# Loading q, k and f of the first three units by token and turning them with full-width transpositions

## The chip, the cores and the metric

The kernel runs on one core of a Trainium2 chip. Its time is the device time of one execution in microseconds; the median of three runs is compared. A profile is one such execution, and its span goes from the first to the last instruction. TensorE (PE) multiplies matrices and writes to PSUM; VectorE (DVE), ScalarE (ACT) and GpSimd (POOL) work on SBUF and PSUM; SyncE (SP) and ACT issue transfers (DMA).

## What is computed

A recurrent attention block is followed by a gated feed-forward block, all in float32:

```
B, H, S, D = 4, 8, 768, 48
f = 1 / (1 + exp(-f_logit))
for t in range(S):
    state = f[:, :, t, :, None] * state + einsum('bhd,bhe->bhde', k[:, :, t], v[:, :, t])
    y[:, :, t] = einsum('bhd,bhde->bhe', q[:, :, t], state)
x = y.transpose(0, 2, 1, 3).reshape(3072, 384)
h = x @ w_in                                  # 384 x 2048
out = (h / (1 + exp(-1.702 * h))) @ w_out     # 2048 x 384
```

## The kernel before

The 4 x 768 tokens are cut into 12 units of 256 tokens (`U`); a unit has two halves of 128 tokens (`HALF`, called f = 1 and f = 0). `attention(n)` builds the work of unit n as a list of parts. `f`, `q` and `k` of a unit come in with token and head dimension in the wrong place: they have to be turned, so that the head dimension (48, in slots of 64) lies on the partitions and tokens lie along the free dimension. The result goes to `F` (the gates) and to slots of `X` (q and k).

In attention, six levels l = 0..5 combine blocks of 1, 2, 4, ... 32 tokens. A level copies keys aside (`set_aside`, tile `Kc`, line 494, ACT), forms scores on PE (`score`, line 425), multiplies q and k by running products of the gates (`promote`, line 519, DVE; the products `tot` are formed on POOL, line 416) and writes masked scores to `A` (lines 466 to 485). `turn_k` (line 595) transposes k back on PE. Then state and output `y` follow (lines 534, 643, 689), `y` is copied to `yT` and sent by DMA to `xT`, which the feed-forward products read (lines 1100 and 1114).

`load_raw(n, j)` loads one of f_logit, q, k (j = 0, 1, 2) into the tile `raw`, which has one place for each j and so is loaded anew only after the turn of the unit before. `turn(j, ...)` turns it. Both have two ways: from unit 3 on (`n >= N_FILL`) DVE transposes blocks of 32 x 32; for units 0, 1 and 2 PE does it. Only the second way is changed.

For those three units a partition of `raw` holds 8 following tokens of one head pair, 384 floats for each of two heads (1536 bytes in a row in memory), one DMA for each of the four head pairs, 32 partitions each. `turn` takes one token of the 8 at a time: for each head a product of 64 columns of `raw` with the identity puts 64 partitions of a PSUM bank, two heads beside each other. A bank holds 4 of the 8 tokens, and ACT evacuates it in two pieces, one for each half, with the tokens written in groups of 4. q is loaded one token early (`first = s0 - 1`), so at the start of a sequence its row 0 has no source and is zeroed.

`opening()` is a hand-written order for unit 0, with pieces of unit 1 between its levels. On SP it issues f, k, the first weights; then f and k for unit 1, v, q for unit 1, more weights. ACT issues q of unit 0. On PE: two products with zeros (`keep_up`, line 125), f, k, q of unit 0, then the levels; f of unit 1 is turned in two pieces at levels 2 and 3 (`next_f`), q and k of unit 1 after `turn_k`. Between levels `keep_up(1)` issues a product whose result nobody reads. ACT runs f's sigmoid, then k's evacuation, `Kc`, q's evacuation. Units 1 and 2 are merged with feed-forward products by `merge`, which interleaves a queue of products with the attention parts by share; the weights are decoded in these units by ACT (line 228) and DVE (lines 230 to 233). SP issues each weight load (line 210) when a buffer comes free.

PE and POOL run in the order in which the code is written; up to unit 2 all engines do (`fill_order`). Later a scheduler orders DVE, ACT and SP.

Of the kernel before, what the change touches and what calls it, by code (L numbers as in the profile page):

```python
# [9 lines left out]
F32 = mybir.dt.float32  # L10
I32 = mybir.dt.int32
U32 = mybir.dt.uint32
AF = mybir.ActivationFunctionType
# [10 lines left out]
def kernel(  # L24
# [33 lines left out]
    nc = tc.nc  # L58
    B, H, S, D = q.shape
    DM = H * D  # L60
    DFF = moe_w_in.shape[1]
    P = 128
# [61 lines left out]
    flat_A = A.rearrange("p c f t -> p (c f t)")  # L124
    keep_up(2, 192, (flat_A[:, :P], flat_A[:, :192]))

    R = U // 32
    RW = R * D + HS - D
    raw = const.tile([P, 3, NP, R * D], F32, name="raw")
    by_pair = [raw.rearrange("p j a x -> p j (a x)")[:, j, :2 * RW].rearrange("p (h x) -> p h x", h=2) for j in range(3)]  # L130
    for j in range(3):
        nc.gpsimd.memset(by_pair[j][:, :, R * D:], 0.0)
    nc.gpsimd.memset(by_pair[1][:1, :, :D], 0.0)
    R4 = HALF // 32
    by_half = raw.rearrange("p j a x -> p j (a x)").rearrange("p j (f a x) -> p j f a x", f=2, a=NP)

    ident = const.tile([P, P], F32, name="ident")
    make_identity(nc, ident)
# [1 line left out]

    masks = const.tile([P, NL - 1, 2, 32], F32, name="masks")
    at = [wp.tile([P, n], I32, tag="bits", name=f"at{j}", bufs=PAIRS_AHEAD) for j, n in enumerate((1, (NL - 1) * 64))]
    nc.gpsimd.memset(by_half[:, :, 1, :, R4 * D - 32:], 0.0)
    nc.gpsimd.iota(at[0], pattern=[[0, 1]], base=0, channel_multiplier=1)
    for l, m in enumerate(LEV[:-1]):
        nc.gpsimd.iota(
# [103 lines left out]
    def load_raw(n, j, engines=(nc.sync,)):  # L250
        if n >= NALL:
            return
        b, s0 = n // NU, n % NU * U
        src = (f_logit, q, k)[j]
        first = s0 - (j == 1)

        def span(head, token, dims, d=0):
            return bass.AP(src.tensor, src.offset + ((b * H + head) * S + token) * D + d, dims)
        if n < N_FILL:
            for a in range(NP):  # L260
                engine = engines[a * len(engines) // NP]
                to = by_pair[j][32 * a:32 * (a + 1), :, :R * D]
                if first < 0 and a == 0:

                    for r, rows in ((1, 16), (17, 15)):
                        engine.dma_start(
                            out=to[r:r + rows], in_=span(0, r * R - 1, [[R * D, rows], [S * D, 2], [1, R * D]])
                        )
                    engine.dma_start(out=to[:1, :, D:], in_=span(0, 0, [[R * D, 1], [S * D, 2], [1, (R - 1) * D]]))
                else:  # L270
                    engine.dma_start(out=to, in_=span(2 * a, first, [[R * D, 32], [S * D, 2], [1, R * D]]))
            return
        for f in (1, 0):
            for r in range(4):
                lo = 32 * (r % 2)
                width = R4 * D - lo
                part = span(r // 2, first + (0 if f else HALF), [[R4 * D, 32], [2 * S * D, NP], [1, width]], lo)
                nc.sync.dma_start(out=by_half[32 * r:32 * (r + 1), j, f, :, :width], in_=part)
            if f and first < 0:
                for r in range(4):  # L280
                    lo = 32 * (r % 2)
                    nc.sync.dma_start(
                        out=by_half[32 * r:32 * r + 1, j, f, :, :D - lo],
                        in_=q[b - 1, r // 2::2, S - 1:S, lo:].rearrange("a t d -> t a d"),
                    )
# [33 lines left out]
    def attention(n):  # L319
# [19 lines left out]
        def turn(j, outs, fn=None, pieces=None):  # L339

            if n >= N_FILL:
# [7 lines left out]
                if fn:  # L349
                    fn()  # L350
                return
            for j0 in pieces or range(0, R, 4):
                pt = bank([P, 4, P], f"t_{n}_{j}_{j0}")
                for jj in range(4):
                    for h in range(2):
                        x = (j0 + jj) * D
                        nc.tensor.matmul(  # L357
                            pt[h * HS:(h + 1) * HS, jj, :], lhsT=by_pair[j][:, h, x:x + HS], rhs=ident, start=True, stop=True
                        )
                for f in (1, 0):  # L360
                    at, step = (j0, 1) if f else (HALF - 1 - j0, -1)
                    nc.scalar.activation(
                        view(outs(f), at, [[HALF, NP], [R * step, 16], [step, 4]]),
                        pt.rearrange("p j (a f i) -> p f a i j", a=NP, f=2)[:, 1 - f],
                        (AF.Tanh if n > 1 else AF.Sigmoid) if fn else AF.Copy, scale=0.5 if fn and n > 1 else 1.0,
                    )
            if fn and n > 1:
                half_up()
# [9 lines left out]
        def begin_f(pieces=None):  # L378
            def decay():
                turn(0, lambda f: F[:, ORDER.index(f) * SLOT:(ORDER.index(f) + 1) * SLOT], sigmoid, pieces)  # L380
            if n > N_FILL + 1 and "moved" in copied:
                with tc.issue_after(copied["moved"].ins):
                    decay()
            else:
                decay()
            if n >= N_FILL or (n == 1 and R - 4 in pieces):
                load_raw(n + 1, 0)

        def begin():
# [880 lines left out]
    def opening():  # L1270
# [18 lines left out]
        for l in range(NL):  # L1289
            chosen[:] = [2, 3][l % 2:][:1]  # L1290
            level(l)
            if l in (2, 3):
                next_f((0, 4)[l - 2:][:1])
            elif l < NL - 1:
                keep_up(1)
            if l == 1:
# [75 lines left out]
```

## Time and profile before

| | |
|---|---|
| runs | 599.06, 598.99, 601.0 us; median 599.06 |
| span of the profiled execution | 594.5 us |
| PE busy | 574.9 us, 97% |
| DVE busy | 429.5 us, 72% |
| ACT busy | 291.9 us, 49% |
| POOL busy | 138.4 us, 23% |
| turns by products, line 357 | 288 records, 5.0 to 68.5 us |
| evacuations of them, line 362 | 36 pieces of 128x256, 383 ns each |
| transpositions, line 595 | 4 records in 0.60 to 0.63 us at 60 us |

Every product in float32 shows as two records of weight load and two of matmul, so 144 products at line 357 give 288 matmul records. The duration of a record includes its way through the array; how far apart records start is the rate. Two products of 64 columns each work on the two halves of the array at a time, so their records start at half the distance of full-width ones.

The profiled execution's time is not listed by itself; its span is 4.56 us below the median of the runs, which also count what lies around the span. An idle engine matters only where the chain of waits passes through it.

### The profile page before, as it was taken

To read this page: it belongs to the slowest core of one execution; us is meant where nothing else is said; L and a number is where in the kernel's file an instruction comes from. 1 tells how busy PE (TensorE), PEld (TensorE's weight loads), DVE (VectorE), ACT (ScalarE), POOL (GpSimd) and SP (SyncE) were. 2 spreads that over 40 slices of the span, in tenths; PEclk is the share of its full clock that TensorE was granted. 3 is DMA by queue.
4 is the path that set the end of the run, shared out by engine and by line. 5 is a ranking of instruction groups with operands and counts; after the bars stand their busy time and mean duration, and the time that the engine had idled before them with its cause. 6 is when DMAs were issued, how large, how long until landed. Compare 5 with 4: busy or idle time off the path is not lost.

```text
span 594.5 us, 18457 instructions
## 1 busy us (share of the span) xinstructions
PE 574.9 (97%) x7814; PEld 513.6 (86%) x7814; DVE 429.5 (72%) x696; ACT 291.9 (49%) x613; POOL 138.4 (23%) x214
## 2 busy tenths in 40 slices
PE   6879899999999999999999999999999999999997
PEld 6756776867768789999999999999999999999897
DVE  2898987964866858789778778786887786462284
ACT  4746643453334353474474474573663564452440
POOL 4031200230027216610610700800700602203000
PEclk9979999999999999999999999999999999999999
DMA  7947859840243552353552343553361211001000
GB/s 181 215 124 179 193 145 225 217 100 1 52 106 66 145 130 65 80 139 77 127 146 51 84 113 91 130 134 60 88 168 44 63 38 29 28 3 27 28 1 27
DMA packets 82834, 58.29 MB, mean 98 GB/s; under 512 B 33153, under 2 KB 74785, under 8 KB 82753
## 3 DMA queue, kind: packets, MB, share of 16 engines
q1 hardware_dynamic: 82416, 56.73, 38.9%
q8 instruction: 61, 1.00, 0.7%
q10 hardware_dynamic: 337, 0.39, 0.3%
q14 instruction: 20, 0.16, 0.1%
HBM read 43.98 MB, written 8.39 MB: 88 GB/s over the span
## 4 chain that ended last, share of the span: by engine, by line
PE 87%; DVE 7%; ACT 3%; issue 1%; DMA 1%; POOL 1%; SPq 0%; DVEq 0%; ACTq 0%
PE h L1006 17%; PE h L1100 13%; PE o_Y L869 11%; PE o L1114 10%; PE o_Z L869 8%; PE h_y L1006 6%; PE sc L425 6%; PE o_X L869 4%; PE o_W L869 4%; PE y L689 2%; PE t L357 2%; PE y L534 2%; PE sc L643 1%; DVE X L519 1%; ACT yT L703 1%
## 5 line engine op out<-in xcount | busy, mean ns | idle before, releaser
L1100 PE MATMUL h<-xT,w_in 128*128 128x256 f32 x384 | 89.6, 388 | 1.4 <-DMA xT<-yT 1.4
L523 DVE TENSOR_TENSOR X<-X,tot 128x1024 f32<-128x1024 f32 x45 | 57.0, 1266 | 39.8 <-PE sc L425 33.2
L1100 PEld LDWEIGHTS h<-xT,w_in 128*128 128x128 f32 x384 | 72.8, 193 | 13.8 <-DMA xT<-yT 2.4
L494 ACT COPY Kc<-X 128x512 f32<-128x512 f32 x72 | 48.4, 672 | 65.7 <-DVE X L523 51.5
L1114 PE MATMUL o<-w_out,g 128*128 128x384 f32 x192 | 65.5, 491 | 0.4 <-DVE w_out L233 0.4
L968 POOL TENSOR_TENSOR E<-xT 128x128 f32<-128x128 f32 (+1 forms) x32 | 17.9, 571 | 204.0 <-DMA xT<-yT 112.0
L1114 PEld LDWEIGHTS o<-w_out,g 128*128 128x128 f32 x192 | 35.4, 190 | 22.8 <-DVE w_out L233 1.0
L1006 PE MATMUL h<-E,w_in 128*128 128x128 f32 (+1 forms) x420 | 53.4, 275 | 0.0
L869 PE MATMUL o_Y<-T,S 128*128 128x192 f32 x288 | 50.6, 329 | 0.0
L1006 PEld LDWEIGHTS h<-E,w_in 128*128 128x128 f32 x420 | 50.1, 192 | 0.0
L1036 ACT ACTIVATE g<-g 128x512 f32<-128x512 f32 (+1 forms) x63 | 35.6, 584 | 26.0 <-DVE g L1034 25.3
L1104 ACT ACTIVATE g<-h 128x256 f32<-128x256 f32 x64 | 23.8, 382 | 49.0 <-PE h L1100 48.6
L869 PEld LDWEIGHTS o_Y<-T,S 128*128 128x128 f32 x288 | 46.8, 190 | 0.5
L1034 DVE TENSOR_TENSOR g<-g,h 128x512 f32<-128x512 f32 (+1 forms) x52 | 31.8, 632 | 14.3 <-PE h L1006 13.3
L485 DVE COPY_PREDICATED A<-masks,sc 128x256 f32<-128x256 uint32 (+1 forms) x98 | 42.0, 506 | 0.1
L703 ACT COPY yT<-y 48x256 f32<-48x256 f32 x88 | 32.2, 366 | 18.3 <-PE y L689 17.2
L372 POOL TENSOR_SCALAR F<-F 128x1024 f32<-128x1024 f32 x10 | 17.2, 1716 | 95.9 <-ACT F L375 84.3
L345 DVE STREAM_TRANSPOSE X<-raw 128x512 f32<-128x512 f32 x36 | 38.1, 1105 | 0.1
L425 PEld LDWEIGHTS sc<-X,Kc 48*64 48x64 f32 x1440 | 26.2, 136 | 11.1 <-ACT Kc L494 4.8
L425 PE MATMUL sc<-X,Kc 48*64 48x64 f32 x1440 | 31.0, 222 | 4.8 <-ACT Kc L494 1.9
L1034 DVE TENSOR_TENSOR g<-g,h_y 128x512 f32<-128x512 f32 (+1 forms) x26 | 16.5, 634 | 22.3 <-PE h_y L1006 21.4
L1025 ACT ACTIVATE g<-h 128x512 f32<-128x512 f32 (+1 forms) x46 | 26.1, 576 | 10.8 <-PE h L1006 10.6
(162 smaller groups left out, 1156.2 us busy)
## 6 DMA issues: line engine op xcount, KB each, us to landing
bits<-in_moe_w_out_dram SPq DMA_DIRECT2D x8, 768.0 KB, 7.2
raw<-in_f_logit_dram SPq DMA_DIRECT2D x48, 96.0 KB, 3.5
raw<-in_k_dram SPq DMA_DIRECT2D x48, 96.0 KB, 3.0
bits<-in_moe_w_in_dram SPq DMA_DIRECT2D x8, 576.0 KB
raw<-in_q_dram SPq DMA_DIRECT2D x44, 96.0 KB, 2.3
k_tok<-z SPq DMA_DIRECT2D x56, 64.0 KB, 1.8
kt<-k_tok SPq DMA_DIRECT2D x14, 256.0 KB, 2.8
out_dram<-osb SPq DMA_DIRECT2D x18, 192.0 KB, 2.7
```

What stands on the lines that cost most here:

```text
L345: nc.vector.transpose(view(out, at, [[HALF, NP], [step, R4], [R4 * step, 32]]), by_half[:, j, f].rearrange("p a (j d) -> p (a j) d", j=R4) ...
L425: nc.tensor.matmul(t["sc"][h][g * HS:(g + 1) * HS, a, s, :], lhsT=t["Kc", l][rows(h), x:x + HS], rhs=rhs(h, a, g), start=True, stop=True,)
L485: moved = nc.vector.copy_predicated(out=view(A, c * HALF + at, dims), mask=mask.bitcast(U32), data=got)
L494: nc.scalar.copy(c.rearrange("p (n two m) -> p n two m", two=2, m=m), view(X, KF * SLOT, [[2 * m, SLOT // (2 * m)], [(KR - KF) * SLOT + m, ...
L523: nc.vector.tensor_tensor(x, x, y, ALU.mult)
L703: nc.scalar.copy(view(yT[rows(h)], at, [[U, NP], [step, HS]]), py[columns(h, g), g, :, f, :])
L869: nc.tensor.matmul(t[name], lhsT=lhs(f), rhs=rhs(f), start=(new and i == 0), stop=(i == HF - 1), skip_group_check=True,)
L1006: nc.tensor.matmul(ph[:, t], lhsT=WA[a][:, f * P:(f + 1) * P], rhs=E[n][b], start=(root and t == 0), stop=not goes_on, skip_group_check=True,)
L1034: nc.vector.tensor_tensor(to, to, part, ALU.add if sign > 0 else ALU.subtract)
L1036: nc.scalar.activation(to, to, AF.Gelu_apprx_sigmoid)
L1100: nc.tensor.matmul(ph, lhsT=w_in[:, c, ff * P:(ff + 1) * P], rhs=xTs[n][:, c, :], start=(c == 0), stop=(c == NK - 1))
L1114: nc.tensor.matmul(t["po"], lhsT=g[ff // FG][:, ff % FG, tt * P:(tt + 1) * P], rhs=w_out[:, ff, :], start=(ff == ffs[0]), stop=(ff == ffs[ ...
```

## The change

For units 0 to 2, a partition of `raw` is now a token. It holds two halves (f) of 8 heads, each head in a slot of 64 floats of which 48 come from memory (192 bytes in a row) and 16 are zeroed once by POOL. A load is two DMAs of 128 partitions x 8 heads x 48, first for half f = 1, then for f = 0; at the start of a sequence q's first one leaves out row 0 and is cut into 112 and 15 rows. With a half, four transpositions of 128 x 128 on PE, two heads each, fill one bank, and the bank is the whole half. It is evacuated in one piece of 128x512, the tokens in order (f = 1) or reversed (f = 0). Evacuations are on ACT as before, but in unit 0 both halves of k and half f = 0 of q are on DVE.

```diff
+    R4 = HALF // 32
+    raw = const.tile([P, 3, 2 * NP * R4 * D], F32, name="raw")
+    by_token = raw[:, :, :2 * H * HS].rearrange("p j (f x) -> p j f x", f=2)
+    by_head = by_token.rearrange("p j f (h d) -> p j f h d", h=H)
     for j in range(3):
-        nc.gpsimd.memset(by_pair[j][:, :, R * D:], 0.0)
-    nc.gpsimd.memset(by_pair[1][:1, :, :D], 0.0)
+        nc.gpsimd.memset(by_head[:, j, :, :, D:], 0.0)
+    nc.gpsimd.memset(by_head[:1, 1, 1, :, :D], 0.0)
...
-    nc.gpsimd.memset(by_half[:, :, 1, :, R4 * D - 32:], 0.0)
+    nc.gpsimd.memset(by_half[:, :, 1, 1:, R4 * D - 32:], 0.0)
...
         if n < N_FILL:
-            for a in range(NP):
-                engine = engines[a * len(engines) // NP]
-                to = by_pair[j][32 * a:32 * (a + 1), :, :R * D]
...
-                    engine.dma_start(out=to, in_=span(2 * a, first, [[R * D, 32], [S * D, 2], [1, R * D]]))
+            for i, f in enumerate((1, 0)):
+                engine, t0 = engines[i % len(engines)], first + (0 if f else HALF)
+                for p0, p1 in ((1, 113), (113, P)) if t0 < 0 else ((0, P),):
+                    engine.dma_start(
+                        out=by_head[p0:p1, j, f, :, :D], in_=span(0, t0 + p0, [[D, p1 - p0], [S * D, H], [1, D]])
+                    )
...
-            for j0 in pieces or range(0, R, 4):
-                pt = bank([P, 4, P], f"t_{n}_{j}_{j0}")
-                for jj in range(4):
-                    for h in range(2):
-                        x = (j0 + jj) * D
-                        nc.tensor.matmul(
-                            pt[h * HS:(h + 1) * HS, jj, :], lhsT=by_pair[j][:, h, x:x + HS], rhs=ident, start=True, stop=True
-                        )
-                for f in (1, 0):
-                    at, step = (j0, 1) if f else (HALF - 1 - j0, -1)
+            for f in pieces or (1, 0):
+                pt = bank([P, NP, HALF], f"t_{n}_{j}_{f}")
+                for a in range(NP):
+                    nc.tensor.transpose(pt[:, a, :], by_token[:, j, f, a * P:(a + 1) * P], ident)
+                to = view(outs(f), *((0, [[HALF, NP], [1, HALF]]) if f else (HALF - 1, [[HALF, NP], [-1, HALF]])))
+                if n == 0 and not fn and (j, f) != (1, 1):
+                    nc.vector.tensor_copy(to, pt)
+                else:
                     nc.scalar.activation(
-                        view(outs(f), at, [[HALF, NP], [R * step, 16], [step, 4]]),
-                        pt.rearrange("p j (a f i) -> p f a i j", a=NP, f=2)[:, 1 - f],
-                        (AF.Tanh if n > 1 else AF.Sigmoid) if fn else AF.Copy, scale=0.5 if fn and n > 1 else 1.0,
+                        to, pt, (AF.Tanh if n > 1 else AF.Sigmoid) if fn else AF.Copy, scale=0.5 if fn and n > 1 else 1.0,
                     )
...
-                next_f((0, 4)[l - 2:][:1])
+                next_f((1, 0)[l - 2:][:1])
```

The order of instructions on PE, and on DVE and ACT but for the replaced ones, stays. On SP two small loads of the last token of q come some 20 issues earlier.

More of the change, by code (lines that the diff above doesn't have):

```diff
@@ L125 @@
     keep_up(2, 192, (flat_A[:, :P], flat_A[:, :192]))
[L127 to L130, printed above, removed]
+    R4 = HALF // 32
+    raw = const.tile([P, 3, 2 * NP * R4 * D], F32, name="raw")
+    by_token = raw[:, :, :2 * H * HS].rearrange("p j (f x) -> p j f x", f=2)
+    by_head = by_token.rearrange("p j f (h d) -> p j f h d", h=H)
     for j in range(3):
-        nc.gpsimd.memset(by_pair[j][:, :, R * D:], 0.0)
-    nc.gpsimd.memset(by_pair[1][:1, :, :D], 0.0)
-    R4 = HALF // 32
-    by_half = raw.rearrange("p j a x -> p j (a x)").rearrange("p j (f a x) -> p j f a x", f=2, a=NP)
+        nc.gpsimd.memset(by_head[:, j, :, :, D:], 0.0)
+    nc.gpsimd.memset(by_head[:1, 1, 1, :, :D], 0.0)
+    by_half = raw.rearrange("p j (f a x) -> p j f a x", f=2, a=NP)
     ident = const.tile([P, P], F32, name="ident")
@@ L142 @@
     at = [wp.tile([P, n], I32, tag="bits", name=f"at{j}", bufs=PAIRS_AHEAD) for j, n in enumerate((1, (NL - 1) * 64))]
-    nc.gpsimd.memset(by_half[:, :, 1, :, R4 * D - 32:], 0.0)
+    nc.gpsimd.memset(by_half[:, :, 1, 1:, R4 * D - 32:], 0.0)
+    assert (NP + 1) * R4 * D <= 2 * H * HS <= (NP + 2) * R4 * D - 32
     nc.gpsimd.iota(at[0], pattern=[[0, 1]], base=0, channel_multiplier=1)
@@ L259, in load_raw @@
         if n < N_FILL:
-            for a in range(NP):
-                engine = engines[a * len(engines) // NP]
-                to = by_pair[j][32 * a:32 * (a + 1), :, :R * D]
[L263 to L267, printed above, removed]
-                        )
-                    engine.dma_start(out=to[:1, :, D:], in_=span(0, 0, [[R * D, 1], [S * D, 2], [1, (R - 1) * D]]))
-                else:
-                    engine.dma_start(out=to, in_=span(2 * a, first, [[R * D, 32], [S * D, 2], [1, R * D]]))
+            for i, f in enumerate((1, 0)):
[4 more added lines that the diff above has]
+                    )
             return
@@ L351, in turn @@
                 return
-            for j0 in pieces or range(0, R, 4):
-                pt = bank([P, 4, P], f"t_{n}_{j}_{j0}")
-                for jj in range(4):
-                    for h in range(2):
-                        x = (j0 + jj) * D
-                        nc.tensor.matmul(
-                            pt[h * HS:(h + 1) * HS, jj, :], lhsT=by_pair[j][:, h, x:x + HS], rhs=ident, start=True, stop=True
-                        )
-                for f in (1, 0):
-                    at, step = (j0, 1) if f else (HALF - 1 - j0, -1)
+            for f in pieces or (1, 0):
[6 more added lines that the diff above has]
+                else:
                     nc.scalar.activation(
-                        view(outs(f), at, [[HALF, NP], [R * step, 16], [step, 4]]),
-                        pt.rearrange("p j (a f i) -> p f a i j", a=NP, f=2)[:, 1 - f],
-                        (AF.Tanh if n > 1 else AF.Sigmoid) if fn else AF.Copy, scale=0.5 if fn and n > 1 else 1.0,
+                        to, pt, (AF.Tanh if n > 1 else AF.Sigmoid) if fn else AF.Copy, scale=0.5 if fn and n > 1 else 1.0,
                     )
@@ L385, in begin_f @@
                 decay()
-            if n >= N_FILL or (n == 1 and R - 4 in pieces):
+            if n >= N_FILL or (n == 1 and 0 in pieces):
                 load_raw(n + 1, 0)
```

## The prediction

> **What bounds the kernel now.** I read the page first, for where TensorE (PE) is short of work.
>
> ```profile
> span 594.5 us, 18457 instructions
> PE   6879899999999999999999999999999999999997
> PEclk9979999999999999999999999999999999999999
> ```
>
> Each digit is a slice of 14.9 us. From the fifth slice on PE is full, so the last 535 us are PE work in a fixed order, none of which the edit touches. Only the first four slices, about 60 us, have room. The edit lies there: nine turns (f, q, k of units 0, 1, 2). What it gains or loses there moves everything behind it by as much. So the next view is the chain of waits of the first 16 us (start, length, what):
>
> ```profile
> 2.12 2.75 DMA raw<-in_f_logit_dram
> 5.00 5.43 PE t L357 x64
> 10.46 0.67 ACT X L362 x2
> 11.15 0.86 ACT Kc L494
> 12.01 1.11 ACT X L362 x4
> 13.16 0.75 PE sc L425 x32
> 14.00 0.70 DVE X L519
> ```
>
> The opening is one chain: issue and landing of f (to 4.87), turns of f and k on PE, evacuation of k, the copy Kc, evacuation of q, first scores at 13.16. That last number is the yardstick for everything below. Next the timeline (start, duration, engine, line), and PE's records at line 357 in two stretches, where the three figures are min/median/max ns:
>
> ```profile
> 0.73 1.81 SPq L271 DMA_DIRECT2D raw<-in_f_logit_dram  x4
> 2.02 1.65 PE L116 MATMUL idle<-A 128*128 128x192 f32 x4 [2.02 <-DVE A L121]
> 5.00 7.17 PE L357 MATMUL t<-ident,raw 128*64 128x128 f32 x96 [1.34 <-DMA raw<-in_f_logit_dram]
> ...
> L357 PE MATMUL t<-ident,raw x28: 421/421/476, 5.0 to 7.8; 128*64 128x128 f32 x28
> ...
> L357 PE MATMUL t<-ident,raw x59: 272/273/273, 8.7 to 11.9; 128*64 128x128 f32 x59
> ```
>
> PE stands still from 3.67 to 5.00 for f. 28 records starting from 5.0 to 7.8 are 104 ns apart; 59 starting from 8.7 to 11.9 are 55 ns apart. The array runs at half rate until about 8.45, though the granted clock reads 1.00 there. Later the same half rate does show as a granted clock, in the table of windows (columns: PE, weight loads, DVE, ACT, POOL busy, then clock):
>
> ```profile
> 35.00:36.00 1.00, 0.00 (x0) 0.00 (x0) 1.00 (x3) 0.98 (x2) 0.00 (x0) 0.92 0.73 163
> 36.00:37.00 1.00, 0.92 (x32) 0.94 (x32) 0.96 (x2) 0.00 (x1) 0.00 (x0) 0.50 0.24 62
> 42.00:43.00 1.00, 1.00 (x4) 0.80 (x4) 0.97 (x2) 0.38 (x1) 0.00 (x0) 0.66 1.08 396
> ```
>
> A clock of 0.92 puts the drop at 35.84 (0.16 us at half), 0.66 the wake at 42.68. The changes at 8.45, 35.84 and 42.68 lie 8 and 2 times 3.42 us apart: the clock is reviewed every 3.42 us on a grid. The stretch 5.03 to 8.45 was all busy and woke it. The one before 42.6 was about 92% busy (idle 39.62 to 39.89) and woke it; the one before that, 1.9 of 3.4 us or 56%, did not.
>
> **The change, step by step.**
>
> *Loads.* f was four DMAs, and the first product needed all: three issues ahead of the last one (0.73 to 2.12), then 2.75 to landing. Now it is two DMAs of 1024 packets of 192 B, and the four transpositions of f's first half need only the first one. v already comes in such packets, so the DMA view of 15.5 to 16.5, in which nothing else flows, prices them; beside it 3 to 5, with today's 1536 B packets:
>
> ```profile
> DMA packets 1083, 0.20 MB, mean 204 GB/s; under 512 B 1083, under 2 KB 1083, under 8 KB 1083
> ...
> DMA packets 384, 0.45 MB, mean 226 GB/s; under 512 B 90, under 2 KB 384, under 8 KB 384
> ```
>
> So 10% less rate, no more. Today's first packets move 1.0 us after the first issue (1.73); 1024 packets at 1083 per us take 0.95, and about 0.7 goes by to the signal (the quickest 96 KB load of `raw` lands 2.2 after issue, of which 1.0 is before the first packet and 0.5 is data). First half of f at 3.4; second at 4.4 to 4.9 (q's queue takes a share from 3.0), needed at 5.4. All 6144 packets of f, k and q are in by 7.4 + 0.7, or 9.6 at 849 per us (28 to 29 us, the rate beside other traffic). SP issues four instead of eight times before the first weights, ACT three instead of six; both queues only get earlier.
>
> *PE.* A bank was 8 half products (16 records, 55 ns apart: 0.88), and is 4 transpositions (8 records). Line 595 already runs this operation: 8 records in 1.09 us, less the last one's 0.27, is 117 ns each, 0.94 a bank; in the chain four take 0.44, 0.88 a bank. So 0 to +0.06 a bank. Six banks in the opening: I take +0.2; the other twelve lie among other PE work, 0.7 at most for the range. At half rate both are 1.71 a bank (16 x 107). PE can now begin at 3.67, directly behind the two idle products that end there, instead of 5.00.
>
> *Evacuation.* A bank was two ACT pieces, 0.66 a pair. It is one of 128x512, 0.585 by line 596's copies. In unit 0 both halves of k and one of q go to VectorE, which today waits 7.64 us up to 12.04 for this chain. A PSUM copy of that width on DVE is not shown: between 0.36 (line 664, 192 wide) and 0.69 (line 519, 512 wide); I take 0.69. The q copy stands ahead of the first products with F on DVE (12.04 today), so these wait for it.
>
> *Sum for the opening.* If the clock wakes at 8.45 as now: f on PE 3.67 to 7.1, k to 9.5, q to 11.25; last q bank out at 11.5, DVE copy to 12.2, first scores at 12.25, a gain of 0.9. If it wakes one review earlier: the stretch 1.62 to 5.03 would hold 1.65 of idle products and 1.36 of transpositions, 88% busy, near the 92% that woke it. Then f ends at 6.1, k at 7.9, q at 9.65; copy to 10.6, first scores 10.65, a gain of 2.5. The grid's position in another execution is not known; PE is busy without a gap from 2.0 instead of 5.0, so on average it wakes 3 us earlier. I take 1.7, the middle.
>
> *After the opening.* The evacuation of unit 1's k is on the chain at 28.72: 1.21 becomes 1.07, gain 0.15. DVE's weight conversion, full from 29.8 to 70, starts earlier by the same amount. Weights are asked for earlier, and q and k for unit 2 land long before use (k issued at 54.9, used at 66.8). Memsets on POOL are larger (three of 128x256: by 0.417 for 128x384, about 0.3 each), which puts the identity at 2.5, covered by the idle products to 3.67; the masks slip to about 5.5, covered by DVE's idle time to 7; with that cover gone, 1 us. Clock reviews fall differently on the thin stretch from 32 to 40: half-rate time there may end up to 2 us earlier or later, 1 us of work either way.
>
> Together: -1.7 - 0.15 + 0.2 = -1.65, a span of 592.85. The median lies 4.56 above the profiled span (599.06 - 594.5); it stays, so **597.4**. Own range: gain 0.9 to 2.5, 0.7 for PE, 1 for the reviews: 595.9 to 599.0.
>
> A rule speaks against this. The Trainium skill, "TensorE: Matmul & The Clock Gate", Part 4: PE-mode transpose, says that transpose mode does not count as PE-busy in the same way and that the full clock does not engage for it. The row above it: line 595's records take 272 ns, as line 357's do when warm, but they ran for about a microsecond among ordinary products, so no row here tells whether they would wake the clock by themselves. By the row the sum is 597.4, by the rule it is the first rival's.
>
> **Rivals.**
>
> 1. *Transpositions do not wake the clock.* It decides if, behind the two idle products, only transpositions run and records stay at the 107 ns step past 8.45. 48 records at 214 from 3.67 end at 13.9; 0.42 and the copy make first scores 15.05, +1.9. Then scores (0.70) and idle products (0.81) double, 1.35 more a level, until ordinary products fill one or two reviews (3.4 to 6.8 us, 1.1 to 2.3 levels): +1.5 to 3.1. Unit 1's q behind the turned k at 22 is 3 us of transpositions more, 0 to +1. Together +3.4 to +6, middle about +4.2: **603.3**. For it: today the clock is woken by ordinary products alone. Against it: PE occupancy is as dense, and scores and k's turn at 22 kept the clock.
>
> 2. *Packets come late.* Nine loads turn into 2048 packets each. For the first half of f to miss even 5.0, they must flow at under 398 per us (1024 in 5.0 - 0.73 - 1.0 - 0.7); the slowest stretch with small packets alone is 542 (17 to 17.5, short of issues). Then no gain, some stall at q: **599.4**.
>
> 3. *Gain is hidden.* First scores earlier, but DVE's conversion waits for weights and PE for xT as before: **599.1**. Against it: DVE is busy 9.7 of 10 us from 50 to 60, and weights wait for DVE, not DVE for them.
>
> **How the numbers follow.** Forecast 0.62, rival 1 0.25, rivals 2 and 3 0.13. Half a per cent, about what a measurement of this kernel can tell from no change, is 3.0 us. Faster by more needs 596.06: the early wake and a lucky review together, 0.19 of the 0.62. Slower by more (602.06) is nearly all of rival 1 and a little of 2: 0.25. The rest, 0.56, is within. The range runs from the forecast's low end, 595.9, into rival 1, to 603.6, which leaves out its upper half.
>
> **What would show it.** Right: first record at line 357's successor near 3.7, scores near 10.7 to 12.3, SP's f issues over by 1.6, DVE copies near 0.69, 8 records of a bank in about 0.9 us once warm. Rival 1: 421 ns records beyond 8.5 until q is through, first scores at 15. Rival 2: PE idle before k or q for DMA. The prediction is wrong if a slice from the fifth on changes, or if the earlier start is lost before 45 us.

## The result and the profile after

The changed kernel takes 600.94 us (median of 20 runs, 597.82 to 602.8) against 598.52 for the kernel before (20 runs, 596.74 to 601.86) on the same chip: a ratio of 1.0031 [1.0016, 1.0046], 1.9 us slower (the ratio is of all runs; the two medians lie 2.4 us apart). The forecast was 597.4.

Two spans need care. The profiled execution of before (594.5) belongs to a run of about 596.6 us: where a run shows both numbers, some 2.1 us lie around a span of before and 1.8 around one of the changed kernel. And the profile after is of the slowest of the 20 runs, 602.8 us. So both kernels were profiled once more; these second profiles (595.2 and 597.2) are read below. Both profiles of before are of quick executions: 596.6 by the same reckoning, and 597.29.

The page after: span; PE busy and granted clock in 40 slices (15.0 us each); engines with their numbers of instructions; the queue that carries PE's code.

```profile
span 601.0 us, 17992 instructions
PE 577.6 (96%) x7598; PEld 513.2 (85%) x7598; DVE 431.0 (72%) x699; ACT 289.1 (48%) x592; POOL 137.8 (23%) x214
PE   5969799999999999999999999999999999999997
PEclk9968989999999999999999999999999999999999
...
q8 instruction: 60, 0.98, 0.7%
```

From the sixth slice on the row of PE is that of before; the fifth reads 7 instead of 8. Most of the loss lies in the first 35 us. In every profile of this study but the two with delayed loads, the span less the start of unit 0's copies to `yT` is 561.8 to 564.7 us (562.3 and 562.4 in the two of before). That start is the yardstick from here on: 32.24 and 32.79 us in the two profiles of before, 37.57 and 34.60 in the two of the changed kernel.

The chain of waits after (start, length, what), which answers to the chain shown of before:

```profile
2.68 7.55 DMA raw<-in_k_dram
...
10.36 2.81 PE t L350 x12
...
13.19 0.70 DVE X L353
...
14.03 1.14 PE sc L416 x32
```

The long piece is no longer PE's turning of f and k (5.43 us) but k's transfer: it lands 7.55 us after its last issue, at 10.22. First scores come at 14.03, not at the forecast's 10.65 to 12.25. PE's timeline shows what PE did meanwhile (start, busy, engine, line, tile, count, and in brackets the idle time before it with its cause):

```profile
4.72 1.09 PE L350 MATMUL t<-ident,raw 128*128 128x128 f32 x4 [1.06 <-DMA raw<-in_f_logit_dram]
6.42 1.12 PE L350 MATMUL t<-ident,raw 128*128 128x128 f32 x4 [0.61 <-DMA raw<-in_f_logit_dram]
8.84 1.11 PE L350 MATMUL t<-ident,raw 128*128 128x128 f32 x4 [1.30 <-DMA raw<-in_k_dram]
10.36 2.79 PE L350 MATMUL t<-ident,raw 128*128 128x128 f32 x12 [0.40 <-DMA raw<-in_k_dram]
```

A bank is 4 records, not 8: a transposition is one record where a product with the identity is two. PE's work in a turn is halved, and PE stands before each of the first four banks for the next half load. k comes late because q's packets, issued by ACT already at 0.91 us, flow beside those of f and k: the last packet on ACT's queue (q10), which carries q, ends at 7.28, while k, which is needed first, lands at 10.22. The DMA view of 4 to 6 us, and that of `q_last` below, where SP alone issues:

```profile
DMA packets 1749, 0.33 MB, mean 165 GB/s; under 512 B 1749, under 2 KB 1749, under 8 KB 1749
...
DMA packets 1793, 0.34 MB, mean 170 GB/s; under 512 B 1793, under 2 KB 1793, under 8 KB 1793
```

That is 875 packets a us, where v's packets alone had shown 1083. With one queue it is 897, so the second queue does not slow the packets; it takes a share of them.

### The profile page after: what moved, and what is told of

Same layout as the page of the kernel before. It is cut to its first block, busy times and chain, and to the rows that moved or that the text cites. A ratio compares the mean times of both kernels' runs of the same rounds, so it can differ in the third digit from the quotient of the medians.

```text
span 601.0 us, 17992 instructions
## 1 busy us (share of the span) xinstructions
PE 577.6 (96%) x7598; PEld 513.2 (85%) x7598; DVE 431.0 (72%) x699; ACT 289.1 (48%) x592; POOL 137.8 (23%) x214
## 4 chain that ended last, share of the span: by engine, by line
PE 88%; DVE 7%; DMA 2%; ACT 1%; issue 1%; POOL 1%; SPq 0%; DVEq 0%; ACTq 0%
PE h L997 17%; PE h L1091 14%; PE o_Y L860 11%; PE o L1105 10%; PE o_Z L860 8%; PE sc L416 7%; PE h_y L997 6%; PE o_X L860 4%; PE o_W L860 4%; PE y L680 2%; PE y L525 2%; PE sc L634 1%; DMA raw<-in_k_dram 1%; PE t L350 1%; DVE A L476 1%
## 5 line engine op out<-in xcount | busy, mean ns | idle before, releaser
L1091 PE MATMUL h<-xT,w_in 128*128 128x256 f32 x384 | 91.0, 394 | 2.2 <-DMA xT<-yT 2.2
L1091 PEld LDWEIGHTS h<-xT,w_in 128*128 128x128 f32 x384 | 74.3, 197 | 14.4 <-DMA xT<-yT 2.4
L416 PEld LDWEIGHTS sc<-X,Kc 48*64 48x64 f32 x1440 | 29.0, 150 | 11.4 <-issue 5.1
L416 PE MATMUL sc<-X,Kc 48*64 48x64 f32 x1440 | 34.1, 238 | 3.2 <-ACT Kc L485 2.1
```

What stands on the lines that cost most here:

```text
L416: nc.tensor.matmul(t["sc"][h][g * HS:(g + 1) * HS, a, s, :], lhsT=t["Kc", l][rows(h), x:x + HS], rhs=rhs(h, a, g), start=True, stop=True,)
L1091: nc.tensor.matmul(ph, lhsT=w_in[:, c, ff * P:(ff + 1) * P], rhs=xTs[n][:, c, :], start=(c == 0), stop=(c == NK - 1))
```

## The experiments

Edits are to the changed kernel unless said otherwise. Ratios are to the kernel before, run beside it (medians 597.88 to 598.52).

| run | median us (runs) | ratio, 95% | start of unit 0's yT |
|---|---|---|---|
| changed kernel | 600.94 (20) | 1.0031 [1.0016, 1.0046] | 37.57 |
| new0 | 602.38 (6) | 1.0070 [1.0049, 1.0090] | 35.49 |
| new12 | 598.66 (12) | 0.9992 [0.9977, 1.0006] | 34.81 |
| halves | 600.15 (8) | 1.0023 [1.0009, 1.0037] | 35.88 |
| twice | 601.44 (6) | 1.0054 [1.0034, 1.0073] | 36.27 |
| q_last | 599.82 (11) | 1.0025 [1.0014, 1.0037] | 35.02 |
| idle | 599.84 (11) | 1.0026 [1.0015, 1.0036] | 35.74 |
| idle_q | 600.38 (12) | 1.0036 [1.0020, 1.0053] | 36.01 |
| best1 | 598.86 (12) | 1.0009 [0.9992, 1.0026] | 36.99 |
| quiet | 603.61 (4) | 1.0089 [1.0060, 1.0118] | 34.36 |
| quiet_before | 602.11 (4) | 1.0070 [1.0055, 1.0085] | 33.12 |
| shift | 598.94 (12) | 1.0032 [1.0010, 1.0055] | 38.69 |
| before_shift | 600.68 (12) | 1.0050 [1.0030, 1.0070] | 34.72 |
| idle_shift | 598.99 (12) | 1.0008 [0.9994, 1.0022] | 34.88 |
| best2 | 598.41 (12) | 0.9999 [0.9981, 1.0016] | 34.62 |
| best3 | 598.45 (12) | 1.0006 [0.9991, 1.0020] | 33.90 |
| best4 | 598.05 (12) | 1.0003 [0.9990, 1.0016] | 32.78 |

The last column is of one execution; a kernel's runs spread over 2 to 6 us, and the profiled one is not always typical (`idle`'s took 600.77, `best1`'s 601.32, the longest of its 12).

### Does a transposition count for the clock, and does its shorter PE time matter?

`halves` keeps the new loads and turns by products of 64 columns again, `twice` issues each transposition two times:

```diff
-                    nc.tensor.transpose(pt[:, a, :], by_token[:, j, f, a * P:(a + 1) * P], ident)
+                    for h in range(2):
+                        x = (2 * a + h) * HS
+                        nc.tensor.matmul(
+                            pt[h * HS:(h + 1) * HS, a, :], lhsT=by_token[:, j, f, x:x + HS], rhs=ident, start=True, stop=True
+                        )
...
-                    nc.tensor.transpose(pt[:, a, :], by_token[:, j, f, a * P:(a + 1) * P], ident)
+                    for _ in range(2):
+                        nc.tensor.transpose(pt[:, a, :], by_token[:, j, f, a * P:(a + 1) * P], ident)
```

> The changed kernel, but each turn by two products of 64 columns with the identity, as before the change; loads and evacuation stay changed. Theory A (the clock: full-width transpositions need half the PE time, and the loads leave gaps, so that no review of 3.4 us in the opening is about 90% busy and the array stays at half rate; a transposition itself counts as work): products last twice as long, PE is dense from 8.8 us on, the clock wakes by 12 to 15 us, first scores at 13 to 14, scores ended by about 23 instead of 26.7; median 598.5 to 599.5. Theory B (transpositions do not count as work): the same, 598.5 to 599.5, as products count. Theory C (the loads: small packets on two queues bring k late, the clock is beside the point): k lands at 10.2 as now, no better than the changed kernel, 600.5 to 601.5.

> The changed kernel with every transposition for units 0 to 2 issued twice into the same place, so that PE's turns last as long as before the change but hold transpositions only. Theory A: like the kernel with half products, the clock wakes by 12 to 15 us; 598.5 to 599.5. Theory B: the clock stays at half rate up to the scores and beyond, turns end about 1.5 us later than in the changed kernel; 602 to 604. Theory C: 600.5 to 602.

PE's records at the transpositions' line in `twice`, in two stretches (ns min/median/max, first and last start):

```profile
L351 PE MATMUL t<-ident,raw x10: 421/421/473, 7.8 to 9.9; 128*128 128x128 f32 x10
L351 PE MATMUL t<-ident,raw x17: 272/273/421, 9.7 to 11.9; 128*128 128x128 f32 x17
```

From 4.74 on only transpositions ran, without a gap that the timeline shows. The last record of 421 ns starts at 9.93, the first of 273 at 10.48, so the full rate came near 10.3 us. So they wake the clock, and the forecast's first rival falls in its mechanism. `twice` is slower all the same: its PE waited 2.56 us inside the products `pd` for nothing that the profile shows ("issue"), a kind of wait that is taken up below. `halves`, with the old PE work and the new loads, still reaches its first scores at 14.01 and is slower than before: the loads set that time, whatever turns the data. By ratios the new loads, with the new evacuation, lose 1.4 us of the 1.9 without any transposition (the two intervals overlap).

### Which units lose?

`new0` changes unit 0 only, `new12` units 1 and 2 only (both layouts side by side, chosen by `n in BY_TOKEN`).

> The change for unit 0 alone; units 1 and 2 are loaded and turned as before the change. Theory A (the clock alone): the opening is that of the changed kernel, with a late wake in many executions, so the loss stays: 600 to 601.5. Theory L (the queue: the small packets of units 1 and 2 fill SP's ring, SP stands still at v's load for 4 to 5.5 us, the second pair of weights lands at 27 to 28 instead of before 25.9 and ACT waits for it ahead of A's evacuation): from 14 us on transfers are those of before, issue of v's load takes 0.4 us, ACT does not wait for weights; what is left is the late wake, 599 to 600.

> The other part alone: unit 0 as before the change, units 1 and 2 loaded by token and turned with transpositions. Theory A: the clock wakes at 8 to 12 us behind unit 0's dense products, as before, so nothing is lost, 598 to 599. Theory L: first scores at 13 as before, but v's load of unit 1 is issued for 4 us and more, ACT waits one to two us for weights at 26 to 28: 599.5 to 600.5.

`new12` cannot be told from the kernel before, and `new0` loses more than the whole change does: the loss needs unit 0. The timeline of `new0`:

```profile
18.64 1.13 PE L448 MATMUL sc<-X,Kc 48*64 48x64 f32 x32
19.71 1.71 PE L369 MATMUL t<-ident,raw 128*64 128x128 f32 x16
21.34 0.69 PE L448 MATMUL sc<-X,Kc 48*64 48x64 f32 x32
```

Scores take 1.13 us instead of 0.69 until 21: the array stayed at half rate, which is put down to PE's gaps before f and k (the next runs fill them).

### Waking the clock, and the order of the loads

`idle` puts six products of zeros, 192 columns, into PE's gaps before and behind the first banks. `q_last` lets SP issue unit 0's q behind f and k. `idle_q` does both, with five such products, `best1` both for a kernel with only unit 0 changed. The edits of `idle` and, behind the last mark, of `q_last`:

```diff
+    HOLD = {(0, 1): 1, (0, 0): 2, (2, 1): 1}
...
+    hold(2)
...
+                if n == 0 and (j, f) in HOLD:
+                    hold(HOLD[j, f])
...
-        load_raw(0, 1, (nc.scalar,))
+        load_raw(0, 1)
```

> The changed kernel with six idle products of 192 columns of zeros put into PE's gaps of the opening (two ahead of f, one and two behind f's halves, one behind k's first half), on a PSUM tile that is free then. Theory A: the array is busy without a gap from 2.0, the clock wakes by 5.4 to 8.8, scores run at full rate from the first level on; first scores still at 13 to 14 as k is late; 596.5 to 598.5, and the runs lie closer together than the 5 us of the changed kernel. Theory B: the idle products are ordinary ones, about half of the busy time, and may or may not wake it: 597 to 601. Theory C: 600.5 to 601.5.

> The changed kernel with q of unit 0 issued on SP behind f and k, not on ACT's queue beside them. Theory C: f and k have the DMA engines to themselves, k lands at about 6.5 to 7.5 instead of 10.2, first scores come at 11 to 12 instead of 14.0, and the loss is gone: 597.5 to 598.5. Theory A: k lands as early, but PE has even less to do before the scores, the clock still sleeps in most executions up to 20 us and later; 599 to 600.5. Theory B: as A.

> The changed kernel with both remedies for the opening: q of unit 0 on SP behind f and k, and five idle products in PE's gaps there. Units 1 and 2 stay changed. Theory A: first scores at 11.5 at full rate in every execution, 1.5 us ahead of before: 597 to 598. Theory L: the lead is lost again at 24 to 33 us to the queue, as in the two single remedies (599.8 each): 599 to 600.

> Both remedies for the opening with the change for unit 0 alone, units 1 and 2 as before the change. Theory L with A for the opening: first scores at 11.5, clock awake, from there transfers as before: 596.8 to 597.8, faster than before the change. If the lead of the opening is hidden behind something else: 598.5.

Both do in the opening what they are for. `idle` reached its first scores at 13.09 at full rate, and its runs lie within 2.2 us of each other instead of 5.0. `q_last` turned k's second half at 7.69 instead of 10.36 and reached first scores at 11.67, 1.5 us ahead of the kernel before. With only unit 0 changed, both together won back the loss: `best1` takes 598.86 where `new0` takes 602.38, and their intervals lie apart. For the changed kernel neither did, and both together were no better (`idle_q`; its interval overlaps that of `best1` slightly). So units 1 and 2 seem to cost something there, although `new12` shows no loss from them alone. The profile of `q_last` says where the lead went:

```profile
7.69 0.63 PE L350 MATMUL t<-ident,raw 128*128 128x128 f32 x4 [0.20 <-DMA raw<-in_k_dram]
...
11.67 0.71 PE L416 MATMUL sc<-X,Kc 48*64 48x64 f32 x32 [0.87 <-DVE X L353]
...
28.28 0.31 PE L525 MATMUL y<-A,vt 64*48 64x64 f32 x2 [0.20 <-ACT A L466]
...
31.30 1.43 PE L525 MATMUL y<-A,vt 64*48 64x64 f32 x43 [1.44 <-issue]
32.93 1.84 PE L680 MATMUL y<-X,st 48*48 48x64 f32 x46 [0.21 <-ACT y L645]
```

In the middle of `y` PE waits 1.44 us for "issue", and behind it the outputs product `y<-X,st` runs at half rate (1.84 us; 1.04 at full rate). ACT had waited 2.00 us for the second pair of weights (2.09 in `idle`; no wait in the two profiles of before). In `idle_q` it waited 2.09 us, and in `best1`, whose units 1 and 2 have the old loads, not at all, which points to the small packets of these units. In `best1` the wait of the kind "issue" was even 3.37 us, inside `pd`.

### A second look at both kernels, and the loads out of the way

> The kernel before, profiled once more, because its profiled execution (span 594.5 us) was shorter than its median of 598 us less the 1.8 us that lie around a span. Common to both theories: the span is the start of unit 2's yT copies plus 474.0 +- 0.4 us. Theory 'lucky' (the first profile showed an unusually early opening): span 596 to 597.5 and unit 0's yT at 33.5 to 35 instead of 32.24, with a longer PE wait of the kind 'issue' than the 0.98 us. Theory 'same opening': yT of unit 0 again within 0.4 us of 32.24 and the missing time between yT of unit 0 and of unit 2 (88.3 us there).

> The changed kernel, profiled once more. If the half clock until 28 us belongs to the change in every execution, sc L416 of the first level again takes over 1.0 us a half level and yT of unit 0 starts at 37 to 38. If it is chance (the review grid of 3.4 us falling otherwise), the first level takes 0.7 us and yT starts at 34 to 35.5, with a span of 596 to 599.5.

`again_before` first, then `again_after`, PE's timeline from unit 0's `y` on, with one earlier row:

```profile
24.40 1.80 PE L357 MATMUL t<-ident,raw 128*64 128x128 f32 x29 [0.53 <-issue]
...
29.11 0.31 PE L534 MATMUL y<-A,vt 64*48 64x64 f32 x2
30.24 1.10 PE L534 MATMUL y<-A,vt 64*48 64x64 f32 x62 [0.82 <-issue]
31.56 1.04 PE L689 MATMUL y<-X,st 48*48 48x64 f32 x46 [0.22 <-ACT y L654]
...
32.49 0.46 PE L425 MATMUL sc<-X,Kc 48*64 48x64 f32 x16
33.81 0.46 PE L425 MATMUL sc<-X,Kc 48*64 48x64 f32 x14 [0.86 <-issue]
```

```profile
29.15 0.81 PE L525 MATMUL y<-A,vt 64*48 64x64 f32 x19 [0.45 <-ACT A L466]
31.78 0.87 PE L525 MATMUL y<-A,vt 64*48 64x64 f32 x43 [1.82 <-issue]
32.86 1.51 PE L680 MATMUL y<-X,st 48*48 48x64 f32 x46 [0.21 <-ACT y L645]
```

In this execution of the changed kernel the clock woke before the first scores, and the first state copy began at 27.65 (27.33 before). Up to there it had lost 0.3 us; the other 1.5 us of the 1.8 at `yT` go here. Three things are to be seen. The waits of before stand in front of the 3rd record of `y` and, 62 + 48 + 18 = 128 records on, behind the outputs, where nothing is late by it; the wait at 24.40 lies 127 records ahead of the first. The wait of the changed kernel stands in front of the 22nd record, 19 behind the two that go first. And it is twice as long.

128 records are one packet of PE's code. The page has 60 packets on queue q8, 16 KB each; 7598 matmul records and as many weight loads are 15196 instructions, and 15196 / 256 is 59.4 (before: 15628 / 256 = 61.05, and 61 packets). The Trainium skill, "Runtime: NRT & Kernel Launch", section "Instruction fetch mechanics", says the same of the size: code comes in blocks of 16 KiB, 256 instructions. It also says that the cost of crossing a block's edge is mostly hidden; the profiles here show 0.4 to 3.4 us at such an edge in the opening. The change takes away 144 records ahead of `y` (72 in unit 0's turns, 24 each in f, q and k of unit 1), which is 128 + 16: edges move by 16 records, to the 19th of `y` by this count, the 22nd in the profile.

The packets of q8 stand in the trace with their times, and they settle what this wait is. In the 20 profiles of this study PE has 23 waits of the kind "issue" that are longer than 0.4 us. Every one of them ends 1.3 to 1.8 us after the end of a packet of code, and stands in front of a record whose number, counted from the start, is 78 to 91 above a multiple of 128. Counting 128 records back gives the time at which PE passed the edge before (us):

| profile | edge before | packet begins | packet ends | PE goes on | wait |
|---|---|---|---|---|---|
| again_before | 24.40 | 27.44 | 28.82 | 30.24 | 0.82 |
| again_after | 22.14 | 28.81 | 30.27 | 31.78 | 1.82 |
| halves | 24.40 | 29.50 | 30.74 | 32.08 | 1.63 |
| idle | 21.13 | 28.74 | 30.14 | 31.69 | 1.91 |

The packet begins 3.0 us behind the edge before in `again_before` and 5.1 to 7.6 us behind it with the new loads. `halves` matters most here, for it has as many records as the kernel before:

```profile
32.08 1.52 PE L529 MATMUL y<-A,vt 64*48 64x64 f32 x59 [1.63 <-issue]
```

Its edge stands in front of the 6th record of `y`, and its wait is still twice that of `again_before`. So, in this one execution, the longer wait comes with the new loads, without any record taken out. In the first profile of the changed kernel, with its late clock, no wait of this kind stands ahead of `yT`: the packet ended at 29.23 and PE came to the edge at 33.52. There the late clock is the loss; in `again_after` it is mostly the late code.

What delays the packet would be the queues: from 28 to 31 us `again_after` moves 2899 packets and `again_before` 801. `quiet` (on `idle_q`) and `quiet_before` put unit 1's v and unit 2's f behind unit 0's outputs:

```diff
-            if n >= N_FILL or (n == 1 and 0 in pieces):
+            if n >= N_FILL:
                 load_raw(n + 1, 0)
...
-            load_v(n + 1)
+            if n:
+                load_v(n + 1)
...
             if n == 0:
                 fetch_weights()
+                load_v(1)
+                load_raw(2, 0)
```

> The changed kernel with idle products and q behind k (as in idle_q, 600.38 us), and in addition the loads of unit 1's v and unit 2's f put behind unit 0's outputs, so that after 24 us nothing stands in the DMA queues before the weights and PE's instructions. Theory J (the lead is lost to full DMA queues): ACT's wait for weights at 27 us falls from 1.8 to 2.1 us below 1.0, PE's wait of the kind 'issue' (1.4 to 3.4 us in the other variants) falls to 1.0 or less, yT of unit 0 starts at 32 to 33.5 instead of 36.0, time 596.5 to 598.5. Rival (the waits have other causes, such as the fetch of PE's instructions by itself): both stay, yT at 35 to 36.5, time 599.5 to 601.

> The kernel before with the same two loads put behind unit 0's outputs, as a control. Theory J: its queues were empty from 30 us on (its profile: DMA share 0 there), so it gains less than quiet does: 597 to 598.5. Rival: unchanged, 598 to 599; if it gains as much as quiet does, the jam does not tell the two kernels apart.

Both became much slower, for a reason that neither expectation had: the delayed loads were themselves too late (in `quiet` PE waited 2.6 us for unit 2's f). Up to unit 0's outputs they can still be compared. `quiet` was 1.65 us earlier than `idle_q` there, with a wait for code of 1.12 us in place of 1.68; `quiet_before` was not earlier than before. The packet began at 27.81 in `quiet` and at 29.02 in `idle_q`. This speaks for full queues as a part of it, by one execution each.

### Moving the edge of the code

`shift` cuts the three idle products of 320 columns between the levels into 4, 4 and 5 over the same columns: 20 more records ahead of `y`. `idle_shift` does the same to `idle` with 2, 1 and 4 (8 records; its edge stood in front of the 10th). `before_shift` cuts those of the kernel before into 5, 5 and 8.

```diff
+    CUT = {0: 4, 1: 4, 4: 5}
+
+    def keep_up_cut(l):
+        pt = bank([P, (NL - 1) * 64], f"idle_{next(serial)}")
+        w = (NL - 1) * 64 // CUT[l]
+        for x in range(0, CUT[l] * w, w):
+            nc.tensor.matmul(
+                pt[:, x:x + w], lhsT=ident, rhs=masks.rearrange("p l f t -> p (l f t)")[:, x:x + w], start=True, stop=True
+            )
...
-                keep_up(1)
+                keep_up_cut(l)
```

> The changed kernel; the three idle products of 320 columns between the levels are cut into 4, 4 and 5 products over the same columns, so that 20 more matmul records go ahead of y and a boundary of 128 records that stood in front of the 22nd record of y stands in front of the 2nd. Theory F: the wait of the kind 'issue' inside y shrinks from 1.82 to 0.9 us or less or falls together with y's wait for ACT's A, the outputs product runs at full rate (1.04), unit 0's yT starts at 33 to 33.9 instead of 34.60, time 1 us or more below the changed kernel: 597.5 to 599.5. Rival (full DMA queues): the wait stays 1.4 us or more wherever the boundary is, yT at 34.3 or later, time 600 to 601.5.

> The kernel before with the same three idle products cut into 5, 5 and 8, 30 more records, so that the boundary that stood behind the outputs (in front of the 17th record of the next unit's scores) falls some 36 records into the outputs product y<-X,st. Theory F: a wait of the kind 'issue' of 0.5 to 0.9 us appears in y<-X,st, yT of unit 0 starts 0.5 to 1 us later than the 32.24 and 32.79 of the two profiles of before, time 598.4 to 599.6. Rival (the place of the boundary does not matter): no more than 0.3 us later, apart from what the cut products themselves add to a level, time 597.5 to 598.4.

> idle (the changed kernel with six idle products in its first turns, 599.84 us), with the level's idle products cut into 2, 1 and 4: 8 more records, so that the code boundary goes from the 10th record of y to the 2nd, where y waits for ACT's A anyway. Theory F: the wait of the kind 'issue' in y (1.91 us) is gone or below 0.6, the outputs product runs at full rate (1.04, not 1.84), unit 0's yT starts at 33 to 34 instead of 35.74, time 598.0 to 599.0. Rival (full DMA queues or fewer records, not the place of the boundary): yT at 35 or later, time 599.5 to 600.3.

`idle_shift` gave the time that was expected of the edge: 598.99 against 599.84 for `idle` (ratios 1.0008 and 1.0026, whose intervals still overlap). `y` in its profile:

```profile
29.50 0.31 PE L545 MATMUL y<-A,vt 64*48 64x64 f32 x2 [2.35 <-ACT A L486]
30.27 2.13 PE L545 MATMUL y<-A,vt 64*48 64x64 f32 x62 [0.45 <-ACT A L486]
32.80 1.84 PE L700 MATMUL y<-X,st 48*48 48x64 f32 x46 [0.40 <-ACT y L665]
```

The wait for code inside `y` is gone. The packet began at 25.04, though, and not at 28.74 as in `idle`: PE passed the edge before at 20.26, just ahead of SP's issue of the second weights (20.36), where `idle` passed it at 21.13, behind that issue (20.46). So the run does not tell the place of the edge from an earlier request for the code. The rest of the expectation missed: outputs still ran at half rate and `yT` began at 34.88, not 33 to 34, because the weights were later still in this execution (ACT waited 3.29 us for them and so held up A).

The runs of `shift` fell into two groups, 598.01 to 599.2 (8 runs) and 602.8 to 603.48 (4). Its profile is of the second, with scores at 1.13 us until the last level at 27.48. The groups lie some 4.6 us apart, which is taken as the price of a late wake (no run of the first group was profiled). In the first group `shift` was where the kernel before is, as expected; the median of all says less. `before_shift` doesn't test the edge: the cut products themselves made each level later (1.33 and 1.98 us instead of 0.81), and the first state copy began at 29.54. The wait expected in the outputs did not come: the packet ended at 32.25, and PE reached that edge at 34.20.

### The last wait, and a faster version

`best2` is `idle_q` with the edge moved and ACT's first step on the second pair of weights emitted behind its copies of A; `best3` also asks for unit 1's q ahead of v; `best4` is `idle_shift` with that ACT step behind unit 0's state products:

```diff
-        begin_pair(1)
-        state["begin"] = 2
         evacuate(NL - 1)
         units[0][1][-2][1]()
+        begin_pair(1)
+        state["begin"] = 2
```

> The changed kernel with idle products against the half clock and q behind k on SP (idle_q, 600.38), its levels' idle products cut into 2, 2 and 4 (10 more records: the boundary from the 12th record of y to the 2nd), and ACT's first step on the second pair of weights put behind its copies of A, so that ACT does not stand 2.1 us before the weights while y waits for A. Theory F with the wait for weights: y starts at 27 to 27.5 instead of 28.90, outputs at full rate, yT of unit 0 at 30.5 to 32 instead of 36.01, time 595.5 to 597.5, below both kernels. Rival: the wait for weights or for code only moves to DVE's conversion and to the first h product, yT at 33.5 or later or the lead lost before the second unit's yT, time 598 to 601.

> best2 (598.41 us) with unit 1's q asked for ahead of unit 0's v instead of behind it. In best2's profile PE waited 0.90 and 3.00 us for that q, and the first state copy began at 29.83. If that wait is what eats best2's early first scores (11.77 us against 13.2 before): q lands before 22 us, the state copy begins at 26 to 27, unit 0's yT at 31 to 32.5, time 595.5 to 597.5, below both kernels. Rival (the queues are full until 28 us whatever the order, so another transfer is late in its stead: v for the products pd, or the weights): yT at 34 or later, time 598 to 599.5.

> idle_shift (598.99 us) with ACT's first step on the second pair of weights emitted behind unit 0's state products instead of ahead of ACT's copies of A. Theory W (the late weights, a transfer behind the many small packets, hold up ACT, and ACT holds up y): y's wait for ACT's A falls from 2.35 to below 0.8, the outputs product runs at full rate (1.04), unit 0's yT starts at 31.8 to 33 instead of 34.88, time 596.5 to 598.0, below idle_shift by 1 us or more and at or below the kernel before. Rival (the weights are needed soon after, so the wait only moves to DVE's conversion and the first h product): yT may be early, but the first h product is not, time 598.6 to 600.

`y` in the profile of `best4`:

```profile
27.42 0.31 PE L545 MATMUL y<-A,vt 64*48 64x64 f32 x2 [0.31 <-ACT A L486]
...
30.70 1.84 PE L700 MATMUL y<-X,st 48*48 48x64 f32 x46 [1.14 <-ACT y L665]
```

`y` starts at 27.42 and `yT` at 32.78, like `again_before`'s 32.79, though the outputs are still at half rate. By ratio `best4` is the kernel before's equal, and its interval ends where the changed kernel's begins: with the clock held, the edge moved and ACT not standing before the weights, the loss is gone (which of the three is worth how much, these runs do not say). The last step alone (1.0008 to 1.0003) is too small to be settled.

No version beat the kernel before. In `best2` and `best3` first scores came at 11.8, 1.4 us early, and the lead went to unit 1's q (3.00 us of waiting in `best2`), and in `best3` to an edge of the code between the levels:

```profile
20.87 0.93 PE L125 MATMUL idle<-masks,ident 128*128 128x80 f32 x4 [1.36 <-issue]
```

PE that is early meets code that is not there yet. The old loads with the new transpositions weren't tried: there the two heads of a token lie in two stretches of `raw`, and one transposition takes its 128 columns from one stretch.

## Why the prediction was wrong

A gain of 1.65 us was forecast and 1.9 us were lost. The step that failed is the landing of the loads, and with it the sum for the opening that was built on it.

- **What bounds the kernel.** Right in the main: from the sixth slice on the row is unchanged (the fifth, read as full, was at 8 already), and what the opening lost reached the end, to within 1 us in the four profiles of the two kernels. `new0` and `twice` lost some 2 us more behind `yT`.
- **Loads.** This step failed first. The sum took the first half of f at 3.4 and k on PE from 6.1 or 7.1, and gave k no landing time of its own. PE began f at 4.72, and k was not in before 10.22, near the far end that the working gave for all three loads (9.6). "So 10% less rate, no more" was off as well, 165 GB/s against 226 before, but the rate is not the point: at 897 packets a us, nearly the same, `q_last` had k's second half on PE at 7.69. k shared the packets with q, which is needed later. "Both queues only get earlier" failed too: single issues of 192-byte packets took SP up to 2.89 us (unit 1's k) and 4.99 us (unit 1's v, at 25.68), the second weights were issued at 19.26 in `again_after` instead of 17.90 in `again_before`, and ACT waited 1.49 us for them, which it did not do before.
- **PE.** "4 transpositions (8 records)" misread two banks as one. A bank takes 0.44 us warm and 0.85 at half rate, half of before, so the step was wrong in the change's favour. It gained nothing: PE was waiting for loads, and with less PE work between the gaps the clock could sleep longer.
- **Evacuation.** Right: DVE's copy took 0.69, ACT's 0.60.
- **Sum for the opening.** First scores at 13.9 and 14.0, not 10.65 to 12.25. The sum put PE without a gap from 2.0; it waited 1.1 to 1.2 us for f and had gaps of 0.2 to 1.3 us before three more banks. The late wake is put down to that: "PE is busy without a gap [...], so on average it wakes 3 us earlier" became later, in some executions not before 28 us, some 4.6 us a time. `q_last` shows the size was within reach (11.67) with another order of loads.
- **After the opening.** "Clock reviews [...] 1 us of work either way" had the right place and no mechanism. Not in the working at all was PE's code: its packets came later with the new loads (`halves`: 1.63 us of waiting inside `y`, with no record taken out), and taking records out moved the edge within `y`. Moving it on was worth about 1.1 us by ratios (`idle` to `idle_shift`), with overlapping intervals, and that run also asked for the code earlier.
- **The median.** The 4.56 us taken as lying around the span were 2.1; the rest was an uncommonly quick profiled execution. Against its own run the forecast gain was 1.65 us from a start 2.5 us too good to be typical.
- **Rivals.** Rival 1 came closest to the late-wake runs (603.3; those of `shift` are 602.8 to 603.5), but by luck, as its mechanism did not hold. The page "TensorE: Matmul & The Clock Gate", Part 4: PE-mode transpose, of the Trainium skill says that transposing does not count as busy in the same way and that the full clock does not engage for it. `twice` disagrees: with nothing but transpositions from 4.74 us on, records went from 421 to 272 ns. What the late-wake profiles show beside them is PE's gaps. Rival 2, late packets, was the mechanism, at 875 packets a us and not under the 398 that it was thought to need: it asked only whether the first half of f would miss 5.0 (PE had it at 4.72) and left k out of the account.

Open: why in the late-wake executions the array stayed at half rate from 14 to 28 us though PE was busy throughout, and how much of the cost at the code's edge is its place in `y` and how much the late packet.

## What to carry to other kernels

Before an operation is made cheaper on an engine, look at what that engine waits for next: here PE's half saved in the turns only uncovered the transfers, and a PE with gaps can wake its clock later. Price every load that the chain needs by its own landing, with all that will flow beside it, and put the one that is needed first alone. When loads are cut into small packets, or instructions taken out ahead of a critical stretch, look where the next block of code begins and when it arrives; waits of the kind "issue" that lie 128 matmul records apart are the sign.

## What was not expected of the hardware

Scores and idle products at half rate did not wake the array. PE's busy time and granted clock in the profile after, in stretches of 3.41 us, laid so that one ends at 28.50, where the rate changes (the prediction worked out 3.42 us for a clock review; columns: length, PE busy with records, clock, DMA share, GB/s):

```profile
8.04:11.45 3.41, 2.21 (x9) 1.00 1.17 228
...
14.86:18.27 3.41, 3.41 (x48) 1.00 1.48 172
18.27:21.68 3.41, 3.41 (x62) 1.00 1.10 169
21.68:25.09 3.41, 3.41 (x57) 1.00 1.00 234
25.09:28.50 3.41, 3.41 (x42) 1.00 1.13 285
```

A stretch at 65% (2.21 of 3.41) did not wake it; between the 56% that did not and the 92% that did in the kernel before, that could be. But three that were full, from 14.86 to 25.09, didn't either; the fourth, with 1.97 us of full-width transpositions, did. The clock column reads 1.00 through all of it: at the start of an execution the half rate shows only in the records' durations.
